# Causal masks of three head pairs by selects on GpSimd, and two memsets moved to GpSimd

## The chip, the cores and the metric

The kernel runs on one core of one Trainium2 chip. The metric is the device time in microseconds of one execution. The engines are TensorE (PE; its weight loads are listed as PEld), VectorE (DVE), ScalarE (ACT), GpSimd (POOL) and SyncE (SP). Each takes its instructions in the order in which the kernel issued them and waits on semaphores for the others. DMAs are issued from the queues of POOL and SP.

## What is computed

Attention with a forget gate over 8 batches, 8 heads, 576 positions and 64 dimensions a head, and then a two-layer network with the activation h - tanh(h) on the 4608 rows that come out:

```
scores = q @ k.T / 8 + (cum[i] - cum[j])        # cum = cumsum(log(f))
scores = where(j > i, -1e9, scores)             # the causal mask
attn   = softmax(scores);  a = attn @ v         # heads side by side: x [4608, 512]
h = x @ w_in;  out = (h - tanh(h)) @ w_out      # w_in [512, 2048], w_out [2048, 512]
```

## The kernel before

A *slot* is one pair of heads `(b, c)` of a batch; slots are numbered `p = 4 b + c`, so 4 to 7 are the pairs (1,0) to (1,3) of batch 1. Batch 0 has a path of its own (`scores0`, `values0`) ahead of slot 4. All engines follow the order in which the program issues (a manual schedule); nothing is reordered. `att_items(p)` lists what a slot issues, and `slot` puts steps of the network (`mlp1`, `mlp2`, `seven`) between the items:

- Seven score tiles, `scores(b, c, ti)`, ti = 0 to 6. Of a tile TensorE makes transposed scores (keys on partitions, queries along the row) for one or two blocks of keys in a bank `ps` (L360). Two banks take turns. ScalarE writes the exponential to an f16 tile `e` (L369); tile 3 goes to one of three tiles `el` that the kernel keeps. Keys later than a query must count for nothing, which matters only in blocks on the diagonal.
- For batch 1 the mask is put on by TensorE: for each diagonal block one more matmul, `neg16` by `tri16`, adds a large negative number to the masked scores in the bank before the exponential (L363). There are ten such matmuls in a pair.
- For batches 2 to 7 POOL puts it on after the exponential: an `affine_select` on `e` writes 0 where the key is later than the query (L379), one for each tile.
- After tile 1 of slot p come the values of the pair before, `values(b, c)` (L388): 30 matmuls, 15 for each of two heads, with blocks of `e` as weights; first those of head a = 0 (tiles 0 to 3), then of a = 1 (tile 3's second half and tiles 4 to 6). VectorE divides by the row sums (L394 to L396), and SP turns the result into `XR` by DMA transposes.
- For pairs up to (2,3), the next pair's q and k are turned by TensorE (`trans`, L256) and copied to `QT` and `KT` (L265). In slot 7 they are issued after tiles 2 and 4 and all their copies are on VectorE.
- `LOADS[(p, ti)]` holds what is issued right behind tile ti of slot p, most of it DMAs from POOL's queue: in slot 5, behind tiles 0 to 4, five loads of v for batch 2 (`load_v`, L95); in slot 7 five loads of q for batch 3 (`load_heads`, L106) and in slot 8 five of k. Ahead of slot 5's, POOL's queue holds the four blocks of `w_out` (L210) and q and k of batch 2 (L214).

The loads of batch 3 fill the tiles `raw[0][1]` and `raw[1][1]` (named qn and kn), which until then hold q and k of batch 1 on partitions 0 to 95. Partitions 96 to 127 of both, 2816 f16 wide, must be zero where the loads don't reach before the tiles are turned. Two memsets do that (L221), issued on VectorE behind tile 5 of slot 6.

Of the kernel before, what the change touches and what calls it, by code (L numbers as in the profile page):

```python
# [22 lines left out]
def kernel(  # L23
# [10 lines left out]
    nc = tc.nc  # L34
    P = 128
# [6 lines left out]
    NPAIR = H // 2  # L42
# [39 lines left out]
    TC = NPAIR * PITCH + LEAD  # L82
# [130 lines left out]
    def load_qk(dst, src, b, h0, h1):  # L213
        nc.gpsimd.dma_start(  # L214
            out=dst[b % 2][:, h0:h1, :, :].rearrange("p h n d -> p h (n d)"),
            in_=src[b, h0:h1, :, :].rearrange("h (p n) d -> p h (n d)", n=NT6))

    LOADS = {(NPAIR, 5): [lambda: load_qk(qn, q, 2, 0, H)],
             (NPAIR, 6): [lambda: load_qk(kn, k, 2, 0, H)]}
    for _, two in raw:  # L220
        LOADS.setdefault((2 * NPAIR - 2, 5), []).append(lambda two=two: nc.vector.memset(two[3 * P // 4:P, 0:TC], 0.0))  # L221
    for i in range(2 * HF):
        LOADS.setdefault((2 * NPAIR + 3 + i // 4, i % 4 * 2), []).append(lambda i=i: weight_sums(i))
    for b in range(2, B):
# [124 lines left out]
    def scores(b, c, ti):  # L349
        ps = ps_sc.tile([P, 512], FP32, tag="sc", name="ps")  # L350
        if ti == LAST:
            e = EL[(b * NPAIR + c) % 3]
        else:
            e = aex.tile([P, 512], FP16, tag="e", name="e")
        lo = min(x[4] for x in TILES[ti])
        hi = max(x[4] + x[3] for x in TILES[ti])
        for a, j, i0, n, col in TILES[ti]:
            h = 2 * c + a
            edge = min(P, n) if b == 1 and i0 == j * P else 0
            nc.tensor.matmul(out=ps[:, col:col + n], lhsT=KT[b % 2][0:D + 3, h, j * P:(j + 1) * P],  # L360
                             rhs=QT[b % 2][0:D + 3, h, i0:i0 + n], start=True, stop=not edge)
            if edge:
                nc.tensor.matmul(out=ps[:, col:col + edge], lhsT=neg16, rhs=tri16[:, 0:edge],  # L363
                                 start=False, stop=True)
            for ib in range(j, NJ):
                w0 = min(ib * P, S - P)
                if i0 <= ib * P < i0 + n:
                    E[(b, h, j, ib)] = e[:, col + w0 - i0:col + w0 - i0 + P]
        nc.scalar.activation(out=e[:, lo:hi], in_=ps[:, lo:hi], func=AF.Exp, scale=qscale)  # L369
        if b == 1:  # L370
            return
        col, cp, step, wd = MASKS[ti]
        view = e[:, col:col + (cp - 1) * step + wd]
        if cp == 1:
            pat = [[1, wd]]
        else:
            view = bass.AP(view.tensor, view.offset, [list(view.ap[0]), [step, cp], [1, wd]])
            pat = [[0, cp], [1, wd]]
        nc.gpsimd.affine_select(out=view, in_=view, compare_op=ALU.is_ge, fill=0.0,  # L379
                                base=0, pattern=pat, channel_multiplier=-1)  # L380
# [223 lines left out]
    def att_items(p):  # L604
        items = []
        here = pairs[p] if p < len(pairs) else None
        before = pairs[p - 1] if NPAIR < p else None
        after = pairs[p + 1] if p + 1 < len(pairs) else None
        for ti in range(len(TILES)):
            if here:  # L610
                items.append((lambda ti=ti: scores(*here, ti), "s%d" % ti))
            for load in LOADS.get((p, ti), ()):
                items.append((load, ""))
            late = 2 * (p == 2 * NPAIR - 1)
            if ti == late and after and after[0] < FAR:
                items.append((lambda: trans(*after, qn, QT, "AV" if after[0] == 1 else "VV"), "q"))
            if ti == 1 and before:
                items.append((lambda: (values(*before), turn(*before)), "v"))
            if ti == 3 + late // 2 and after and after[0] < FAR:
                items.append((lambda: trans(*after, kn, KT, "VV"), "k"))  # L620
        return items
# [157 lines left out]
```

## Time and profile before

| | |
|---|---|
| median of 3 runs | 349.9 us (349.33 to 353.63) |
| the profiled execution | 350.76 us, its span 349.1 us, mean granted TensorE clock 0.993 |
| TensorE busy | 337.2 us, 97% of the span |
| VectorE, ScalarE, POOL busy | 238.6, 222.8 and 150.7 us (68%, 64%, 43%) |
| matmuls of L363 (masks by TensorE in slots) | 40, 7.5 us busy |
| selects of L379 on e and el (masks by POOL) | 168, 56.9 us busy |
| memsets of L221 on VectorE | 2, 1.23 us each |

Busy times of matmuls overlap each other, since one starts while the one before it is still draining; what a matmul costs TensorE is the distance from its start to the next one's. The slots of batch 1 start (tile 0's scores) at 33.16, 39.88, 46.94 and 53.99 us and slot 8 at 64.58 us from the start of the span. Idle time of an engine counts only where something on the path to the end waits for it.

### The profile page before, as it was taken

The page shows a single profiled execution, that of the slowest core. Times are in us where ns is not written, and L with a number is a line of the kernel's source. Part 1 is how long each engine was busy: PE and PEld are TensorE (multiplying, and loading weights), DVE is VectorE, ACT ScalarE, POOL GpSimd, SP SyncE. Part 2 cuts the span into 40 slices and gives each one's busy share as a digit, 9 for nine tenths or more (in the row PEclk, how much of TensorE's full clock was granted, in tenths as well). Part 3 has the DMA queues.
Part 4 walks back from the last instruction along what each step waited for, and adds up shares of the span by engine and source line. Part 5 has one row for each costly group of instructions (what it writes and reads, how often), then busy time and mean ns, then how long its engine had stood idle before and what let it go on. Part 6 is the DMA issues. An engine that isn't in the chain of part 4 may idle for free.

```text
span 349.1 us, 8719 instructions
## 1 busy us (share of the span) xinstructions
PE 337.2 (97%) x3384; PEld 236.6 (68%) x3384; DVE 238.6 (68%) x483; ACT 222.8 (64%) x417; POOL 150.7 (43%) x291
## 2 busy tenths in 40 slices
PE   6889997999999999999999999999999999999995
PEld 3878884555555556888887568655887787477475
DVE  6588889446973399547863786378647965975973
ACT  4787885356765688468756875688568843633631
POOL 8964513355267644665477547662222220000000
PEclk9999999899999999999999999999999999999999
DMA  9999999999989999999999999999430013012002
GB/s 88 141 201 187 203 179 159 138 128 198 173 116 147 178 190 158 119 164 157 178 184 178 167 171 181 176 177 176 106 109 20 17 50 109 0 32 91 0 32 90
DMA packets 161323, 45.96 MB, mean 132 GB/s; under 512 B 141506, under 2 KB 159234, under 8 KB 161282
## 3 DMA queue, kind: packets, MB, share of 16 engines
q0 software_dynamic: 100128, 18.36, 74.6%
q1 hardware_dynamic: 61074, 26.99, 39.5%
q8 instruction: 26, 0.43, 0.5%
q14 instruction: 15, 0.12, 0.1%
q10 hardware_dynamic: 80, 0.07, 0.1%
HBM read 36.85 MB, written 9.44 MB: 133 GB/s over the span
## 4 chain that ended last, share of the span: by engine, by line
PE 87%; DVE 6%; ACT 3%; DMA 2%; issue 1%; ACTq 0%; DVEq 0%
PE hps L464 31%; PE cx L505 14%; PE ps L360 10%; PE cz L505 10%; PE ops L583 8%; PE av L388 7%; PE hps L450 3%; DMA XR<-xn 2%; DVE gt L417 2%; PE ps L302 2%; ACT e L307 1%; DVE KT L265 1%; PE t L274 1%; PE t L256 1%; ACT th L416 1%
## 5 line engine op out<-in xcount | busy, mean ns | idle before, releaser
L464 PE MATMUL hps<-XR,win 128*128 128x512 f16 (+4 forms) x640 | 125.9, 336 | 0.8 <-DMA XR<-xn 0.6
L369 ACT ACTIVATE e<-ps 128x512 f16<-128x512 f32 x168 | 98.6, 594 | 43.9 <-PE ps L360 40.8
L417 DVE TENSOR_TENSOR gt<-hps,th 128x512 f16<-128x512 f32 x144 | 98.4, 688 | 39.3 <-ACT th L416 38.1
L416 ACT ACTIVATE th<-hps 128x512 f32<-128x512 f32 x144 | 86.1, 598 | 29.6 <-PE hps L464 20.6
L379 POOL TENSOR_SCALAR_AFFINE_SELECT e<-e 128x128 f16<-128x128 f16 x144 | 49.2, 341 | 102.5 <-ACT e L369 101.5
L464 PEld LDWEIGHTS <-win 128*128 128x128 f16 x640 | 56.3, 97 | 43.7 <-issue 0.5
L360 PE MATMUL ps<-QT,KT 67*128 67x512 f16 (+1 forms) x336 | 70.3, 279 | 0.5 <-ACT e L369 0.5
L505 PEld LDWEIGHTS <-gt 128*128 128x128 f16 x560 | 52.5, 97 | 8.2 <-DVE gt L417 0.4
L360 PEld LDWEIGHTS <-KT 67*128 67x128 f16 x336 | 32.5, 99 | 22.3 <-issue 1.7
L95 POOL DMA_DIRECT2D vn<-in_v_dram x40 | 34.4, 862 | 10.5 <-DMA win<-in_moe_w_in_dram 2.2
L583 PE MATMUL ops<-wout,gt 128*128 128x512 f16 x128 | 33.4, 386 | 0.0
L388 PEld LDWEIGHTS <-e 128*128 128x128 f16 x784 | 28.0, 97 | 3.3
L498 DVE TENSOR_TENSOR snap<-cz,snap 128x512 f32<-128x512 f32 x21 | 14.5, 691 | 22.4 <-PE cz L505 7.4
L388 PE MATMUL av<-vn,e 128*128 128x65 f16 x784 | 29.2, 193 | 0.0
L505 PE MATMUL cz<-wout,gt 128*128 128x256 f16 x224 | 27.8, 272 | 0.0
L106 POOL DMA_DIRECT2D qn<-in_q_dram x25 | 21.2, 850 | 10.6 <-PE ps L363 8.8
L396 DVE TENSOR_TENSOR xn<-av,rs 128x640 f16<-128x640 f32 x28 | 23.1, 825 | 1.0
L505 PEld LDWEIGHTS <-sw 128*128 128x128 f16 x224 | 21.1, 97 | 3.9
L106 POOL DMA_DIRECT2D kn<-in_k_dram x25 | 21.3, 853 | 1.4 <-issue 1.4
L542 ACT ACTIVATE snap<-cx 128x512 f32<-128x512 f32 (+1 forms) x16 | 8.7, 544 | 16.2 <-PE cx L505 16.2
L583 PEld LDWEIGHTS <-gt 128*128 128x128 f16 x128 | 11.3, 98 | 10.6 <-issue 0.8
L307 ACT ACTIVATE e<-ps 128x512 f16<-128x512 f32 x25 | 14.3, 596 | 4.5 <-PE ps L305 2.5
(108 smaller groups left out, 383.1 us busy)
## 6 DMA issues: line engine op xcount, KB each, us to landing
vn<-in_v_dram POOLq DMA_DIRECT2D x32, 128.0 KB, 7.0
out_dram<-ost SPq DMA_DIRECT2D x14, 256.0 KB
out_dram<-snap SPq DMA_DIRECT2D x14, 256.0 KB
qn<-in_q_dram POOLq DMA_DIRECT2D x24, 128.0 KB, 5.0
kn<-in_k_dram POOLq DMA_DIRECT2D x24, 128.0 KB, 4.6
QT<-TQ SPq DMA_DIRECT2D x10, 288.0 KB
KT<-TK SPq DMA_DIRECT2D x10, 288.0 KB
win<-in_moe_w_in_dram POOLq DMA_DIRECT2D x2, 1024.0 KB, 11.4
```

The source lines that it names most:

```text
L95: nc.gpsimd.dma_start(out=dst[0:pn, n, h0:h1, 0:D], in_=src[b, h0:h1, n * P:n * P + pn, :].rearrange("h p d -> p h d"))
L106: nc.gpsimd.dma_start(out=to, in_=src[b, :, n * P:n * P + pn, :].rearrange("h p d -> p h d"))
L360: nc.tensor.matmul(out=ps[:, col:col + n], lhsT=KT[b % 2][0:D + 3, h, j * P:(j + 1) * P], rhs=QT[b % 2][0:D + 3, h, i0:i0 + n], start=True ...
L369: nc.scalar.activation(out=e[:, lo:hi], in_=ps[:, lo:hi], func=AF.Exp, scale=qscale)
L379: nc.gpsimd.affine_select(out=view, in_=view, compare_op=ALU.is_ge, fill=0.0, base=0, pattern=pat, channel_multiplier=-1)
L388: nc.tensor.matmul(out=av[:, a, ib, :], lhsT=E.pop((b, 2 * c + a, j, ib)), rhs=vn[b % 2][:, j, 2 * c + a, 0:D + 1], start=(j == 0), stop=( ...
L396: nc.vector.tensor_tensor(out=xn.rearrange("p i (a d) -> p a i d", a=2), in0=av[:, :, :, 0:D], in1=rs.to_broadcast([P, 2, NJ, D]), op=ALU. ...
L416: nc.scalar.activation(out=th, in_=hps, func=AF.Tanh, scale=-1.0)
L417: nc.vector.tensor_tensor(out=to, in0=view(hps), in1=view(th), op=ALU.add)
L464: nc.tensor.matmul(out=hps[:, o:o + n], lhsT=win[:, ci, ft * P:(ft + 1) * P], rhs=XR[:, ci, t:t + n], start=(ci == 0), stop=(ci == NCH - 1))
L505: nc.tensor.matmul(out=ps, lhsT=stationary(u, LHS[ph], ft, m), rhs=moving(RHS[ph], ft), start=fresh and ft == 0, stop=(ft == HF - 1), skip ...
L583: nc.tensor.matmul(out=ops, lhsT=GT[(u, ft, m)], rhs=wout[:, ft, :], start=(ft == 0), stop=(ft == NFT - 1))
```

## The change

Pair (1,0) keeps its masks by TensorE. In pairs (1,1), (1,2) and (1,3) the 30 matmuls of L363 go, and 21 selects on POOL, one for each tile, come behind the exponentials, as in the later batches. The two memsets are issued on POOL, behind tile 5 of slot 5, not on VectorE behind tile 5 of slot 6; in the built program they are 32x2816 f16 on POOL and were 32x1408 uint32 on VectorE.

```
@@ LOADS
     for _, two in raw:
-        LOADS.setdefault((2 * NPAIR - 2, 5), []).append(lambda two=two: nc.vector.memset(two[3 * P // 4:P, 0:TC], 0.0))
+        LOADS.setdefault((2 * NPAIR - 3, 5), []).append(lambda two=two: nc.gpsimd.memset(two[3 * P // 4:P, 0:TC], 0.0))
@@ scores(b, c, ti)
             h = 2 * c + a
-            edge = min(P, n) if b == 1 and i0 == j * P else 0
+            edge = min(P, n) if (b, c) == (1, 0) and i0 == j * P else 0
...
         nc.scalar.activation(out=e[:, lo:hi], in_=ps[:, lo:hi], func=AF.Exp, scale=qscale)
-        if b == 1:
+        if (b, c) == (1, 0):
             return
```

POOL's order in the changed kernel around slot 5, as built: select of tile 0, load of v, select of tile 1, load, select of tile 2, load, select of tile 3, load, select of tile 4, load, select of tile 5, memset of qn, memset of kn, select of tile 6; then the seven selects of slot 6 with nothing between them; and in slot 7 the first five selects each followed by a load of q.

More of the change, by code (lines that the diff above doesn't have):

```diff
@@ L220 @@
     for _, two in raw:
-        LOADS.setdefault((2 * NPAIR - 2, 5), []).append(lambda two=two: nc.vector.memset(two[3 * P // 4:P, 0:TC], 0.0))
+        LOADS.setdefault((2 * NPAIR - 3, 5), []).append(lambda two=two: nc.gpsimd.memset(two[3 * P // 4:P, 0:TC], 0.0))
     for i in range(2 * HF):
@@ L358, in scores @@
             h = 2 * c + a
-            edge = min(P, n) if b == 1 and i0 == j * P else 0
+            edge = min(P, n) if (b, c) == (1, 0) and i0 == j * P else 0
             nc.tensor.matmul(out=ps[:, col:col + n], lhsT=KT[b % 2][0:D + 3, h, j * P:(j + 1) * P],
@@ L369, in scores @@
         nc.scalar.activation(out=e[:, lo:hi], in_=ps[:, lo:hi], func=AF.Exp, scale=qscale)
-        if b == 1:
+        if (b, c) == (1, 0):
             return
```

## The prediction

> **What bounds the kernel now.** I read the page's busy shares first, then the chain of waits between 40 and 70 us, where slots 5 to 7 run, and then the timelines of POOL and TensorE there.
>
> ```profile
> PE 337.2 (97%) x3384; PEld 236.6 (68%) x3384; DVE 238.6 (68%) x483; ACT 222.8 (64%) x417; POOL 150.7 (43%) x291
> ```
>
> TensorE is busy for 97% of the span, so a microsecond counts where it falls into TensorE's order. The chain is TensorE's own from 40 to 51 us and then leaves it:
>
> ```profile
> 54.65 0.35 issue
> 55.00 1.23 DVE qn L221
> 56.23 0.24 issue
> 56.47 1.23 DVE kn L221
> 57.70 0.03 issue
> 57.73 0.69 DVE gt L417
> ...
> 60.32 0.81 DVE QT L265
> 61.13 0.14 issue
> 61.26 0.64 PE t L256 x6
> ```
>
> The reader should see the two memsets of L221 ahead of a gate, a normalisation and two copies on VectorE; TensorE's transposes wait for those copies. The timeline of TensorE gives the price, and the table of windows the clock (the column after POOL's):
>
> ```profile
> 61.26 0.64 PE L256 MATMUL t<-id,kn 96*128 96x96 f16 x6 [2.41 <-DVE QT L265]
> 61.70 0.57 PE L360 MATMUL ps<-QT,KT 67*128 67x448 f16 x1
> ```
> ```profile
> 61.20:64.60 3.40, 3.33 (x18) 1.89 (x19) 1.59 (x2) 1.19 (x2) 0.79 (x2) 0.50 2.47 147
> ```
>
> TensorE stands idle for 2.41 us, and then its granted clock is 0.50 for 3.4 us. The same stretch of work (61.26 to 64.58) is worth 1.57 us less at full clock: six transposes 0.44 against 0.26 at 50.88, the next tiles 1.17 against 0.62 at 52.50, four matmuls of L583 1.71 against 0.87.
>
> POOL looks idle in slots 5 and 6, but its order isn't free. This is its timeline (start, length, idle before and the guessed releaser):
>
> ```profile
> 40.19 0.88 POOL L95 DMA_DIRECT2D vn<-in_v_dram  x1 [0.41 <-PE x L336]
> 42.72 0.87 POOL L95 DMA_DIRECT2D vn<-in_v_dram  x1 [1.65 <-PE hps L450]
> 45.26 0.87 POOL L95 DMA_DIRECT2D vn<-in_v_dram  x1 [1.67 <-DMA wout<-in_moe_w_out_dram]
> 47.80 0.69 POOL L95 DMA_DIRECT2D vn<-in_v_dram  x1 [1.67 <-PE t L256]
> ```
>
> The last three start 2.54 us apart. In the built program each load on POOL's queue waits for the landing of the eighth load before it; for these three that is the first three blocks of wout. The releasers named are mostly guesses; the even spacing is that of landings. In the kernel before nothing else stands behind these loads.
>
> **The change part by part.** *Removed from TensorE:* ten matmuls of L363 in each of three pairs, eight of 128 columns and two of 64. TensorE's timeline has 0.057 us from the start of the first kind to the next matmul's, 0.033 from the second's: 24 x 0.057 + 6 x 0.033 = 1.6 us at most.
>
> *Removed from VectorE:* the memsets. Without them the copies of QT wait only for their transposes: these are issued by 2.7 us after slot 7's first tile, the result is there 0.2 later, two copies take 1.6, so the next transposes start at 4.65 where they now start 7.27 after that tile (53.99 to 61.26). That is 2.6 us with 0.2 of masks in it, or 2.4 of stall, of which I call 0.1 left over; the half clock goes with it. Gain 2.3 + 1.6 = 3.9 us.
>
> *Added to POOL:* 21 selects (L379 rows: 308 ns for 128 columns, 408 for 256, 320 in el), 7 a pair, some 2.4 us; and the two memsets in slot 5, behind tile 5's select and ahead of tile 6's. The loads of vn keep their places, so the selects of slot 5 now stand between and behind them, and the values of pair (1,1), in slot 6, wait for tile 6's select. Follow POOL. Tile 2's exponential ends at 43.77 on ScalarE's timeline, so its select near 44.4; the third load (its landing came at 42.7) and tile 3's select follow; the fourth load waits until 45.26 and ends near 46.4; tile 4's select follows; the fifth load can't start before 47.80 and ends at 48.49; tile 5's select ends at 48.80. Then come the memsets.
>
> Their price no row shows. The build keeps them as 32x2816 f16 on POOL, where VectorE has 32x1408 uint32:
>
> ```profile
> L221 DVE MEMSET qn<- 32x1408 uint32 x1 | 1.2, 1232 | 0.3 <-issue 0.3
> ...
> L717 POOL MEMSET el<- 128x192 f16 x3 | 0.9, 320 | 0.0
> ```
>
> Below, VectorE's own 1.23 us each. Above, the slope between POOL's memset of 192 elements (320 ns) and those of one (98 to 101): 1.15 ns an element, 3.34 us each. The slope of the selects (100 ns for 128 more) would give 0.32 + 2624 x 0.78 ns = 2.4. I take 2.8, between the two POOL slopes, since both are rows of the engine that does the work: 5.6 us for the two. Tile 6's select then ends at 48.80 + 5.6 + 0.41 = 54.8, and TensorE goes on at about 54.95.
>
> [...]
>
> In the kernel before, the matmul that needs tile 6 is the 21st of 30 in the group that starts at 47.76, 0.0304 us apart: 48.37. So that point is late by 54.95 - 48.37 = 6.6 us. The masks removed up to there gain nothing, for TensorE only waits longer. TensorE takes its instructions in order, so all behind it is late too; vector and scalar engines run dry. After 7 us of idleness I expect the half clock again, as after 2.41: 1.57 us more; none and twice that (two such stretches) are the bounds. The masks left after that point (18 of 30): 0.9 us gained.
>
> Tile 6 of pair (1,2) is not late: from its issue, exponential and select need about 2.1 us and TensorE reaches its use after 2.5. The five q loads of slot 7 cost POOL 4.2 us and its selects 2.4, from 0.9 after the slot's start; pair (1,3)'s values come some 10 us after that start (67.88 - 53.99, less the 3.9). These loads lose their wait on the VectorE memset (8.79 us idle before the first), which no longer matters as the slot itself is 8 us later.
>
> **Sum:** +6.6 + 1.6 - 0.9 - 3.9 = +3.4 us. The profiled execution took 350.76 us (span 349.1, 1.7 around it), near the median of 349.9; a difference made in the span carries over: 349.9 + 3.4 = 353.3 us, 1% slower, which is within the 2% that a measurement of this kernel can about tell from no change.
>
> **The rivals.** *A, POOL is not late.* If tile 6's select came in time, both gains would stand whole: 1.6 + 3.9 = 5.5, or 344.4 us. For it speaks POOL's 43%; against it the load at 47.80, the memsets behind it and values that begin at 47.76. It would need wout landing some 7 us sooner. *B, cheap memsets.* At 1.23 us each the delay is 3.5 us instead of 6.6: +0.3, or 350.2 us. For it speaks that the engine might write two f16 at a time; against it the 320 ns. *C, slower: the stall comes twice.* In slot 7 the five q loads stand between the selects of pair (1,3), whose values leave POOL a slack of about 10 - 0.9 - 6.6 = 2.5 us. If these loads wait for landings as the three of slot 5 do (1.65 each, 8.3 for five), TensorE waits 5.8 us more and the clock falls again (1.57): +10.8, or 360.7 us. It decides once the waits pass 2.5 us in all, and is over 2% from 4.5 on. For it speaks that the loads eight back are large (two of 576 KB, 18.1 and 20.8 us to landing) and the DMA queues full; against it that by then, near 62 us, those issued at 37 to 48 us have had their 11 to 21 us. *D, the memsets cost more than any row says:* from 4.6 us each the whole passes 2% (357 us).
>
> **How the numbers follow.** Forecast (350.5 to 356.5) 0.62; A 0.06; B 0.12; C 0.10; D 0.10. The range leaves out most of A, C and part of D: 350 to 357.5. Its ends are B's 350.2 and the upper memset (+1.1) with two half-clock stretches (+1.6) and a little beside. Faster by over 2% is 342.9 or less, past even A: 0.02. Slower by over 2%, C, D and the forecast's tail: 0.21. Within 2%: 0.77.
>
> **What would show it.** Right: on POOL, memsets of qn and kn from about 48.8 us, 2.4 to 3.3 us each; TensorE idle at L388, waiting for POOL's e of L379, for 6 to 7.5 us from about 47.5; a clock of 0.50 after it; no 2.4 us wait for QT before the transposes of slot 7; L363 at 10 matmuls. Wrong: no wait at L388 (A); memsets near 1.2 us (B); a second wait at L388 some 18 us later (C); the half clock absent, or the wait before L256 still there. The sum would fall if the fifth load of slot 5 started well before 47.8.

## The result, and the profile after

The changed kernel takes 354.07 us (median of 20 runs, 352.9 to 355.46) against 350.69 us (348.69 to 354.04) of the kernel before in 20 runs beside it. The ratio is 1.0095, with a 95% interval of 1.0072 to 1.0118: about 3.3 us slower. Its profiled execution took 354.93 us with a span of 353.2 us, at the upper end of its runs.

First the waits of the kernel after, who waited for whom (us in total, times, the longest); no wait at L388 stood there before:

```profile
PEld L388 <- POOL e L379: 7.3, 2, 5.2
PE av L388 <- POOL e L379: 7.1, 2, 5.1
```

TensorE waits twice, 7.1 us in all, at the values of pair (1,1): 1.98 us for POOL's select of tile 5 and 5.09 us for that of tile 6. POOL's timeline shows why:

```profile
46.38 0.89 POOL L95 DMA_DIRECT2D vn<-in_v_dram  x1 [1.14 <-DMA wout<-in_moe_w_out_dram]
47.28 0.30 POOL L379 TENSOR_SCALAR_AFFINE_SELECT e<-e 128x128 f16<-128x128 f16 x1
48.81 0.69 POOL L95 DMA_DIRECT2D vn<-in_v_dram  x1 [1.22 <-DMA wout<-in_moe_w_out_dram]
49.49 0.30 POOL L379 TENSOR_SCALAR_AFFINE_SELECT e<-e 128x128 f16<-128x128 f16 x1
49.86 2.44 POOL L221 MEMSET qn<- 32x2816 f16 x1
52.24 2.44 POOL L221 MEMSET kn<- 32x2816 f16 x1
54.75 0.90 POOL L379 TENSOR_SCALAR_AFFINE_SELECT e<-e 128x256 f16<-128x256 f16 x3
```

Read it downwards: the fourth and the fifth load of v each wait for a block of wout to land; tile 5's select, the two memsets and tile 6's select follow the fifth without a gap. The same values on TensorE in the kernel before, where nothing is waited for:

```profile
47.76 0.58 PE L388 MATMUL av<-vn,e 128*128 128x65 f16 x14
48.22 0.58 PE L388 MATMUL av<-vn,e 128*128 128x65 f16 x14
```

And in the kernel after, with the wait in brackets, and the table of windows (the clock stands third from the right):

```profile
49.86 0.26 PE L388 MATMUL av<-vn,e 128*128 128x65 f16 x3 [1.98 <-POOL e L379]
55.21 0.67 PE L388 MATMUL av<-vn,e 128*128 128x65 f16 x9 [5.09 <-POOL e L379]
...
62.73 0.61 PE L360 MATMUL ps<-QT,KT 67*128 67x512 f16 x3 [0.28 <-DVE KT L265]
```
```profile
48.50:55.00 6.50, 0.26 (x3) 0.14 (x3) 0.80 (x1) 0.48 (x2) 6.06 (x5) 0.83 1.40 187
55.00:58.00 3.00, 2.79 (x23) 2.18 (x24) 1.21 (x3) 0.31 (x1) 0.65 (x3) 0.50 2.56 157
58.00:62.00 4.00, 4.00 (x36) 3.15 (x35) 2.22 (x4) 2.85 (x7) 0.95 (x3) 0.80 1.58 78
```

The restart at 55.21 falls into a half clock that lasts to about 59.6 (0.20 missing of the 4 us from 58 on is 0.8 us, which at half clock takes 1.6 us). The 2.41 us wait for QT before L256 in slot 7 is gone.

Where the time went, from slot 4's first scores to slot 8's, in three pieces:

| piece | before | after | difference |
|---|---|---|---|
| slot 4's start to the matmul that needs tile 6 of (1,1) | 48.37 - 33.16 = 15.21 | 55.21 - 32.98 = 22.23 | +7.0 |
| from there to slot 7's start | 53.99 - 48.37 = 5.62 | 62.73 - 55.21 = 7.52 | +1.9 |
| slot 7 | 64.58 - 53.99 = 10.59 | 69.51 - 62.73 = 6.78 | -3.8 |
| together | 31.42 | 36.53 | +5.1 |

The spans differ by 4.1 only. From slot 8 on this execution of the kernel before took 0.8 us longer than that of the kernel after (349.1 - 64.58 = 284.5 against 353.2 - 69.51 = 283.7); it has a wait for XR (0.6 us before L464, from 218.69 us on in its chain) that the kernel after has not. The last 0.2 are in the start of slot 4.

### The profile page after: what moved, and what is told of

It is laid out like the page before. It is cut to its first block, busy times and chain, and to the rows that moved or that the text cites. A ratio compares the mean times of both kernels' runs of the same rounds, so it can differ in the third digit from the quotient of the medians.

```text
span 353.2 us, 8688 instructions
## 1 busy us (share of the span) xinstructions
PE 336.0 (95%) x3354; PEld 235.4 (67%) x3354; DVE 236.6 (67%) x481; ACT 222.6 (63%) x417; POOL 162.0 (46%) x314
## 4 chain that ended last, share of the span: by engine, by line
PE 80%; DMA 10%; POOL 5%; DVE 2%; issue 1%; ACT 1%; POOLq 0%; ACTq 0%
PE hps L464 30%; PE cx L505 14%; PE cz L505 10%; PE ps L360 10%; PE ops L583 8%; PE av L388 7%; DMA vn<-in_v_dram 6%; DMA wout<-in_moe_w_out_dram 4%; DVE KT L265 1%; POOL vn L95 1%; PE hps L450 1%; POOL kn L99 1%; POOL qn L99 1%; DVE gt L417 1%; POOL qn L221 1%
## 5 line engine op out<-in xcount | busy, mean ns | idle before, releaser
L464 PE MATMUL hps<-XR,win 128*128 128x512 f16 (+4 forms) x640 | 125.7, 336 | 0.2
L369 ACT ACTIVATE e<-ps 128x512 f16<-128x512 f32 x168 | 98.5, 594 | 40.1 <-PE ps L360 38.7
L379 POOL TENSOR_SCALAR_AFFINE_SELECT e<-e 128x128 f16<-128x128 f16 x162 | 55.2, 342 | 105.3 <-ACT e L369 104.8
L464 PEld LDWEIGHTS <-win 128*128 128x128 f16 x640 | 56.3, 97 | 43.7 <-issue 0.5
L360 PE MATMUL ps<-QT,KT 67*128 67x512 f16 (+1 forms) x336 | 69.0, 278 | 1.3 <-DVE KT L265 0.7
L505 PEld LDWEIGHTS <-gt 128*128 128x128 f16 x560 | 52.5, 97 | 8.2 <-DVE gt L417 0.4
L388 PE MATMUL av<-vn,e 128*128 128x65 f16 x784 | 29.8, 193 | 7.1 <-POOL e L379 7.1
L388 PEld LDWEIGHTS <-e 128*128 128x128 f16 x784 | 28.4, 97 | 10.9 <-POOL e L379 7.3
L583 PE MATMUL ops<-wout,gt 128*128 128x512 f16 x128 | 32.6, 378 | 0.0
L394 DVE TENSOR_SCALAR rs<-av 128x10 f32<-128x10 f32 x28 | 4.5, 161 | 23.8 <-PE av L388 23.8
L450 PE MATMUL hps<-XR,win 128*128 128x256 f16 x128 | 18.2, 290 | 0.3 <-DVE gt L417 0.3
```

What stands on the lines that cost most here:

```text
L388: nc.tensor.matmul(out=av[:, a, ib, :], lhsT=E.pop((b, 2 * c + a, j, ib)), rhs=vn[b % 2][:, j, 2 * c + a, 0:D + 1], start=(j == 0), stop=( ...
L464: nc.tensor.matmul(out=hps[:, o:o + n], lhsT=win[:, ci, ft * P:(ft + 1) * P], rhs=XR[:, ci, t:t + n], start=(ci == 0), stop=(ci == NCH - 1))
L505: nc.tensor.matmul(out=ps, lhsT=stationary(u, LHS[ph], ft, m), rhs=moving(RHS[ph], ft), start=fresh and ft == 0, stop=(ft == HF - 1), skip ...
L583: nc.tensor.matmul(out=ops, lhsT=GT[(u, ft, m)], rhs=wout[:, ft, :], start=(ft == 0), stop=(ft == NFT - 1))
```

## The experiments

The theory (Q): what counts is POOL's order. Tile 6's select stands behind the loads of v, one of which waits for a landing, and behind two memsets; TensorE waits for it, and falls to half clock. Rival S: selects between exponential and values cost by themselves, wherever POOL stands. Rival M: the stall in slot 7 was not the memsets' doing. Each ratio is against the kernel before on the same chip, with its 95% interval, and a difference in us is the ratio's. The kernel before scatters between 348.5 and 354.0 us, so a difference of medians can be somewhat larger or smaller.

**e1_masks_only**: the masks as changed, the memsets back on VectorE.

```
-    ...setdefault((2 * NPAIR - 3, 5), []).append(lambda two=two: nc.gpsimd.memset(...))
+    ...setdefault((2 * NPAIR - 2, 5), []).append(lambda two=two: nc.vector.memset(...))
```

> The masks of the three pairs go to POOL, the memsets stay on VectorE in slot 6. My theory (the select of slot 5's tile 6 waits for the landing ahead of the fifth load of v and, above all, for the two memsets): without memsets on POOL that select ends near 49.2 to 50.2 us, so the values of pair (1,1) are late by 1 to 2 us, not 6.6; two short waits at L388 of some 2 us in all, with or without half a clock (0 to 1.6), 0.9 gained by the masks left; the wait of 2.4 us before L256 in slot 7 is still there or a little shorter. Sum 0 to +2.5 us against the kernel before. Rival S (the selects themselves, standing between exponential and values, are what costs): the delay stays about as long as in the changed kernel, and the 3.9 us that the memsets gave back are gone: +5 to +7.

Measured: ratio 1.0046 (1.0016 to 1.0076), +1.6 us. From its timeline of TensorE:

```profile
48.92 0.80 PE L388 MATMUL av<-vn,e 128*128 128x65 f16 x12 [0.17 <-POOL e L379]
58.06 0.38 PE L360 MATMUL ps<-QT,KT 67*128 67x512 f16 x1 [0.43 <-ACT e L369]
62.00 0.64 PE L256 MATMUL t<-id,kn 96*128 96x96 f16 x6 [2.69 <-DVE QT L265]
```

The wait at L388 shrinks from 7.1 to 0.17 us, even less than I expected, so S falls. The stall of slot 7 is back, and a little longer; the half clock after it lasts longer too (below). Slot 4 to slot 8 takes 31.10 us, 0.3 less than before, but the half clock goes on for 2.8 us of slot 8, which is 1.4 us lost: +1.1 of the +1.6. The rest this profile doesn't place.

**e2_memsets_only**: the memsets on POOL in slot 5, all masks of batch 1 left to TensorE.

> The memsets go to POOL in slot 5, all masks of batch 1 stay on TensorE. My theory: nothing on TensorE's order waits for POOL then, so the memsets' 2 x 2.44 us there cost nothing, and the stall of 2.4 us with its half clock in slot 7 goes: -3 to -4 us, no wait at L388. Rival S expects the same. Rival M (the stall in slot 7 comes from the landing of k of batch 2 or from the copies, not from the memsets on VectorE): the wait before L256 stays, 0 to -0.5.

Measured: ratio 0.9921 (0.9889 to 0.9952), -2.8 us (medians 346.96 against 350.07), a little under the -3 to -4 expected, which the interval reaches. No wait at L388 or before L256; slot 4 to slot 8 takes 27.90 us and not 31.42. M falls: the stall was the memsets'. The transposes of slot 7 on TensorE, and POOL:

```profile
58.93 0.42 PE L256 MATMUL t<-id,kn 96*128 96x96 f16 x6
61.05 0.39 PE L360 MATMUL ps<-QT,KT 67*128 67x512 f16 x1 [0.22 <-DVE KT L265]
```
```profile
48.75 2.44 POOL L221 MEMSET qn<- 32x2816 f16 x1
51.13 2.44 POOL L221 MEMSET kn<- 32x2816 f16 x1
```

The memsets are those of the changed kernel, at the same place in POOL's order: 4.8 us of POOL's time that cost nothing where no select that TensorE waits for stands behind them.

**e3_u32**: the changed kernel with `two.bitcast(mybir.dt.uint32)[3 * P // 4:P, 0:TC // 2]` cleared instead.

> The changed kernel with the same bytes cleared as uint32, 1408 elements a row and not 2816. If POOL's memset takes its time by element (2.44 us for 2816, 320 ns for 192: 0.81 ns each, 0.16 fixed), each takes 1.3 us, the select of tile 6 is ready 2.3 us sooner, and the time is 2.3 us less than the changed kernel's: +1 against the kernel before. If it goes by bytes, 2.44 us each and +3.4 as before.

Measured: ratio 1.0067 (1.0042 to 1.0092), +2.3 us: less than the changed kernel by 1.0 us, where 2.3 were expected, and the intervals overlap. The rows settle the price, groups of POOL with busy time and mean ns:

```profile
L221 POOL MEMSET qn<- 32x1408 uint32 x1 | 1.3, 1266 | 0.1
L221 POOL MEMSET kn<- 32x1408 uint32 x1 | 1.3, 1266 | 0.0
```

Half the elements for the same bytes, 1266 ns and not 2440: here POOL's memset took its time by element. TensorE restarts 4.06 us behind the start of the fifth load (48.11 to 52.17) where the changed kernel has 6.40 (48.81 to 55.21): 2.3 us less, as worked out. Why the time fell by less is not settled by these runs alone: 1.0 us by the ratios, 1.7 us by the medians (352.38 against 354.07). The half clock is still there.

**e4_early**: the changed kernel with the memsets issued far ahead, one behind the memsets of `el`, one before the loads of `w_out`.

```
     for e in EL:
         nc.gpsimd.memset(e, 0.0)
+    nc.gpsimd.memset(raw[0][1][3 * P // 4:P, 0:TC], 0.0)
...
+    nc.gpsimd.memset(raw[1][1][3 * P // 4:P, 0:TC], 0.0)
     for t in range(0, NFT, 4):
```

> The changed kernel with the two memsets issued on POOL far ahead, one behind the memsets of el and one before the loads of w_out, where POOL waits for a landing anyway. My theory: the delay of pair (1,1)'s values shrinks to that of e1, 1 to 2 us, with or without half a clock, and the 3.9 us of the stall in slot 7 are gained: -3.5 to -0.5 us against the kernel before. Rival S: the delay stays, +2 to +3.4. If the memsets push the loads of w_out back instead, all landings of slot 5 are up to 1 us later and with them the values: 1 us more.

Measured: ratio 0.9946 (0.9913 to 0.9978), -1.9 us. No wait at L388 at all: with the memsets away, the selects among the loads of v are in time. Slot 4 to slot 8 takes 27.44 us, 0.5 less than in e2; yet the kernel is not faster than e2, and in its profile slot 4 starts at 35.25 us, the latest of all. TensorE's last wait there, 0.57 us, is for a DMA into KT. That the early memsets delayed the loads ahead of slot 4 fits this, but other kernels with that part unchanged start anywhere from 32.98 to 34.58, so it is not shown.

**e5_v_later**: the changed kernel with the loads of v for batch 2 in slot 6, so that no load stands among slot 5's selects.

```
-            LOADS.setdefault((p0 + 1, n), []).append(lambda b=b, n=n: load_v(b, n))
+            LOADS.setdefault((p0 + 1 + (b == 2), n), []).append(lambda b=b, n=n: load_v(b, n))
```

> The changed kernel with the five loads of v for batch 2 issued a slot later (slot 6), so that no load stands among the selects of slot 5. My theory (what sets the time is the landing that the fifth load waits for, and then the memsets): tile 5's select is done near 46.8 us, the memsets end near 51.7, TensorE goes on near 52.2 and not 55.2: 3 us less than the changed kernel, 0 to +1 against the kernel before, the half clock still there. Rival L (the landings don't matter, POOL is late by its own work): no difference to the changed kernel, +3.4. The five loads cost POOL 4.3 us in slot 6; if they make pair (1,2)'s selects late, a second wait at L388 shows it.

Measured: ratio 1.0054 (1.0025 to 1.0083), +1.9 us; a miss of my 0 to +1 and of L's +3.4. Its memsets start right behind tile 5's select (48.07 in its profile, slot 4 at 34.58), and TensorE restarts 19.2 us after slot 4's start: 4.0 late, as worked out. My base was one execution: in the changed kernel's first profile, with its 7.0, the fifth load starts 15.8 us after slot 4, later than in every other profile with these loads in slot 5 (13.2 to 15.0). e9 has another.

**e6_two_pairs**: masks by POOL for pairs (1,2) and (1,3) alone (`b == 1 and c < 2` where the change has `(b, c) == (1, 0)`), and the memsets as uint32.

> Masks by POOL for pairs (1,2) and (1,3) alone, pair (1,1) stays with TensorE; the memsets on POOL in slot 5 as uint32 (1.27 us each). My theory: no select stands behind the loads of v, the memsets end near 51.3 us, before pair (1,2)'s selects are urgent, so there is no wait at L388 and no half clock: -3.5 to -4.2 us against the kernel before, 0.3 to 1 better than the memsets alone. Rival S (selects between exponential and values cost by themselves): no better or worse than the memsets alone, -2.8 or less.

Measured: ratio 0.988 (0.9836 to 0.9924), -4.2 us (medians 347.04 against 350.23), with no wait at L388 and the clock at 1.00 from slot 5 to slot 8. Faster than both kernels; the interval overlaps e2's, and the medians are 347.04 and 346.96. So the 20 matmuls that it saves over e2 buy nothing that these runs can tell.

**e7_no_masks**: the changed kernel without any causal mask in the three pairs.

```
-        if (b, c) == (1, 0):
+        if b == 1:
             return
```

> The changed kernel with no causal mask at all in pairs (1,1) to (1,3), neither matmuls nor selects (the attention of these six heads is not causal); the memsets on POOL in slot 5. It shows what the 30 matmuls are worth where nothing waits for POOL. By the distances on TensorE's timeline 1.6 us: -5 against the kernel before, 1.6 below the memsets alone. If ScalarE and VectorE pace the slots of batch 1, as the 0.3 us a slot in the changed kernel's profile suggest, 0.3 a slot or 1 us: -4.2.

Measured: ratio 0.9881 (0.984 to 0.9921), -4.2 us, as the second estimate had it; but the interval overlaps e2's, and the median of 347.01 us is no better than those of e6 or e2. In the profiles slot 4 to slot 8 takes 27.60 us against 27.90 in e2, so there 30 matmuls are worth 0.3 us, 10 ns each and not the 53 ns on average that I had counted. Its timeline of TensorE shows where the rest stays:

```profile
45.54 1.03 PE L450 MATMUL hps<-XR,win 128*128 128x256 f16 x8 [0.26 <-DVE gt L417]
52.66 1.03 PE L450 MATMUL hps<-XR,win 128*128 128x256 f16 x8 [0.64 <-DVE gt L417]
58.41 0.38 PE L360 MATMUL ps<-QT,KT 67*128 67x512 f16 x1 [0.37 <-ACT e L369]
61.89 0.39 PE L360 MATMUL ps<-QT,KT 67*128 67x512 f16 x1 [0.40 <-DVE KT L265]
```

TensorE saves the matmuls and then waits for VectorE's gates and copies and ScalarE's exponentials: 1.7 us of waits, where e2 has 0.5 (0.30 and 0.22 before the last two of these). In e2 the masks fill the rest.

**e8_warm**: the changed kernel with 26 matmuls on a tile of ones ahead of pair (1,1)'s values (`spin(26 * (before == (1, 1)))`).

> The changed kernel with 26 matmuls of 512 columns on a tile of ones ahead of pair (1,1)'s values, whose results nobody reads: about 5.6 us of work inside the stall of 7. My theory (1.6 to 2.1 us of the loss are the half clock after the stall): the clock stays at 1.00 and the time is 1.5 to 2 us under the changed kernel's: +1.4 to +1.9 against the kernel before. Rival K (the slower work after the stall has another cause, such as empty buffers to be filled again): no difference, +3.4.

Measured: ratio 1.0057 (1.0025 to 1.0089), +2.0 us, 1.2 to 1.3 under the changed kernel, where 1.5 to 2 were expected (by the medians 1.7, 352.39 against 354.06). The clock stays up:

```profile
53.00:56.00 3.00, 2.94 (x47) 2.28 (x46) 0.99 (x3) 0.19 (x1) 1.33 (x4) 1.00 1.73 184
56.00:60.00 4.00, 3.73 (x38) 2.91 (x35) 3.27 (x6) 3.73 (x9) 1.28 (x5) 1.00 2.43 135
```

From the matmul that needs tile 6 to slot 7's start it takes 5.44 us (54.43 to 59.87) against 7.52 in the changed kernel: the half clock costs 2.1 us there. The added matmuls end at 53.8, the 20 matmuls of the values that don't need tile 6 come next, and so TensorE reaches the one that does at 54.43, 0.5 us after tile 6's select is done (53.50 + 0.41); this explains part of the shortfall. K falls by the trace: the same work takes 2.1 us less at full clock. By the ratios alone it would not, for their intervals overlap.

**e9_changed_again**: the changed kernel once more, for a second profile.

> The changed kernel once more, beside the next one, for a second profile of it. In the profiles so far the start of the fifth load of v lies 13.7 to 15.8 us after slot 4's first scores (15.8 in the changed kernel's own profile, 14.6 in the kernel before). If TensorE's restart hangs on that landing, the distance from slot 4's start to the restart is this distance plus 6.3 to 6.4 us: 20 to 21.4 for 13.7 to 15, so 5 to 6 us late, not 7.0; +3.4 us against the kernel before. If the landing doesn't matter the distance is 22.2 as before, whatever the load does.

Measured: ratio 1.0091 (1.0053 to 1.0128), +3.2 us. POOL:

```profile
47.74 0.69 POOL L95 DMA_DIRECT2D vn<-in_v_dram  x1
48.43 0.30 POOL L379 TENSOR_SCALAR_AFFINE_SELECT e<-e 128x128 f16<-128x128 f16 x1
48.79 2.44 POOL L221 MEMSET qn<- 32x2816 f16 x1
```

Slot 4 started at 34.41 us, so the fifth load comes 13.3 us after it, with no wait; TensorE restarts at 54.14, 6.4 us behind the load as expected, and 19.73 after slot 4's start. The wait is 4.80 us, and the pieces are +4.5, +2.0 and -3.8: +2.7 together. Of the 3.2 us between the spans (352.3 and 349.1) another 1.3 lie ahead of slot 4, which the change doesn't touch, and 0.7 come back behind slot 8's start. So one profile beside another shows the pieces, and only the many runs show what the change is worth in all.

**e10_v_later_warm**: e5 with 16 such matmuls ahead of pair (1,1)'s values.

> Loads of v a slot later, and 16 matmuls on a tile of ones (3.5 us) ahead of pair (1,1)'s values. If the terms add up: 4 us late for the memsets alone, no half clock, 3.4 gained in slot 7 and 0.3 by the masks: +0.3 us against the kernel before, 2 to 2.5 under the version with the later loads alone (+2.7), 3 under the changed kernel. If the half clock is not the rest of the loss: +2 or more.

Measured: ratio 1.0012 (0.9978 to 1.0046), +0.4 us, slot 4 to slot 8 in 31.51 us against 31.42. With the loads out of the way and the clock kept up, what the memsets take (4 us late) just equals what their leaving VectorE gives (pieces +4.0, -0.2 and -3.7). The terms add up.

## Why the prediction was right, point by point

The forecast was 3.4 us slower, 353.3 us; measured were 3.3 us, 354.07 us, inside the range. The mechanism is the one forecast: fifth load, memsets, tile 6's select, TensorE's order, half clock, and the gain in slot 7. That the sum came within 0.1 us is luck: the terms' errors cancel in part, and with the measured terms the two profiles of the changed kernel add up to +5.1 and +2.6.

| term | predicted | measured |
|---|---|---|
| two memsets on POOL | 5.6 us | 4.8 (start to start 2.38, each 2.44) |
| TensorE late at tile 6 | +6.6 | +7.0 and +4.5 in two profiles |
| half clock after it | +1.6 | 2.1 (e8 against the changed kernel's profile) |
| masks left after that point | -0.9 | -0.5 (e8 against e2, both at full clock: 5.44 + 6.78 against 5.62 + 7.06) |
| stall and half clock of slot 7 | -3.9 | -3.8 (slot 7), -3.5 (slots 4 to 8 in e2), -2.8 in e2's time |

- *The memsets' price* was a middle of two slopes; the lower one (2.4) was right, with 2.44 measured for each. In e3 the same bytes as uint32 took POOL about half the time (1.27 us).
- *The landing.* I took the fifth load's start, 47.80 us, as fixed. It lay from 47.56 to 48.81 in the profiles, and slot 4's start varies from 32.98 to 35.25. The delay is the distance between the two: where slot 4 starts early, TensorE gets further ahead and waits longer; where it starts late (e9), the fifth load doesn't wait at all and POOL's own work sets the time. That is why two profiles have +7.0 and +4.5, and waits of 7.1 and 4.8 us where 6 to 7.5 were forecast. The later loads of e5 restart TensorE 19.2 us after slot 4's start, half a microsecond sooner than e9: in an execution like e9's the loads among the selects cost no more than that.
- *The masks* were costed by the distance of starts on TensorE's timeline. This step failed: it holds where TensorE is the only bound, and VectorE and ScalarE are nearly full too (busy 6.1 and 5.9 of the 7 us between 40 and 47 us before). About half of the 0.9 came, and e7 shows the freed time turning into waits.
- *The half clock.* I took one stretch as in the kernel before, with two as the bound. In the changed kernel two come, the first in part inside the stall (clock missing: 6.5 x 0.17 + 3 x 0.50 + 4 x 0.20 = 3.4 us, or 6.8 at half clock).
- *Rivals.* A (POOL in time) fell with the wait of 7.1 us. B (cheap memsets) fell at 2.44 us; e3 made a kernel with B's price, 1.27, and it was still slower than the kernel before, so B's +0.3 was too low by 2 us. C (a second stall) didn't come: slot 7's loads of q start 1.2 us apart, without a wait for a landing. D (dearer memsets) didn't come either.

## What to carry to other kernels

Before work is moved to an engine that looks idle, read the order of that engine's queue: here POOL's loads, one of them tied to a landing, stood ahead of the selects, and memsets that were free while nobody waited for POOL (e2) held TensorE up by most of 4.5 to 7.0 us once it did. The effects of two edits need not add: the memsets alone gained 2.8 us, the masks alone lost 1.6, and together they lost 3.3 and did not gain 1.2. And what an instruction costs on the busiest engine need not be what its removal saves, where other engines are nearly as full: 10 ns a matmul in e7, not the 53 counted.

## What the hardware showed beyond that

In the six profiles read here (the kernel before, the changed kernel's two, e1, e3 and e5) the half clock at the stall lasts about 3.4 us or twice that. In the kernel before, a wait of 2.41 us is followed by one such stretch (from about 61.2 to 64.6). In e1 a wait of 2.69 us at the same place is followed by two; the windows of e1:

```profile
60.00:62.00 2.00, 0.00 (x1) 0.03 (x1) 1.84 (x3) 0.00 (x0) 2.00 (x4) 0.73 1.93 125
62.00:64.00 2.00, 2.00 (x12) 1.22 (x13) 1.31 (x2) 0.84 (x2) 1.37 (x4) 0.50 1.98 120
64.00:66.00 2.00, 2.00 (x6) 0.73 (x5) 0.29 (x1) 0.53 (x2) 0.53 (x2) 0.50 2.22 136
66.00:68.00 2.00, 2.00 (x12) 1.02 (x10) 0.15 (x1) 0.91 (x2) 1.19 (x2) 0.56 0.10 5
```

The missing clock is 2 x (0.27 + 0.50 + 0.50 + 0.44) = 3.4 us, at half clock 6.8 us, of which 5.8 fall on work. So 0.3 us more of waiting went with twice the slow time.

The length of the wait need not be what decides. The clock missing from the windows, taken as half clock, puts the fall of the clock 0.1 us ahead of TensorE's restart in the kernel before (61.17 and 61.26). It is 1.1 us ahead in e1 (60.9 and 62.00), 2.5 and 2.3 in the changed kernel's two profiles (52.74 and 55.21, 51.8 and 54.14), 1.2 in e3 (51.0 and 52.17) and 1.6 in e5 (52.2 and 53.78), and all five have 6.8 to 6.9 us of half clock, two stretches. So in these five, where a microsecond or more of the first stretch passed without a matmul, a second followed each time. Nor does the clock fall after a fixed idle time here: about 2.3 us after the end of TensorE's last matmul in the kernel before, about 1.6 us in e1. And not every execution of the kernel before has such a stretch: 9 of the 69 that ran beside the experiments have a mean clock of 0.998 or more, so at most 0.7 us missing, where one stretch at half clock is 1.7.

That the place of the fall decides between one stretch and two is read from these six profiles; no run here varies it by itself.
